# One decode step: a quarter of the scores of the first and the last head pair on TensorE, one load for w_mod, another order of work at the end

## The chip, the cores and the metric

One NeuronCore of one Trainium2 chip runs the whole program. The metric is the time of the execution on the device in microseconds (us). The kernel before took 685.55 us in the median of 3 runs (685.35 to 686.33).

## The reference: what is computed

A block for one token: adaptive layer norm, attention over a cache of 16384 keys and values for each of 32 heads of width 128, and a SwiGLU feed-forward part (width 640, inner width 1728). The core of it:

```python
mod = (silu(c) @ w_mod).reshape(1, 6, 1, 640)       # sa, ca, ga, sb, cb, gb
h = layernorm(x) * (1 + ca) + sa
q = (h @ wq) as 32 heads of 128
scores = q . k_cache[head] * 128 ** -0.5             # 32 x 16384
o = softmax(scores) @ v_cache[head]
x = x + ga * (o @ wo)
h = layernorm(x) * (1 + cb) + sb
x = x + gb * ((silu(h @ w_gate) * (h @ w_up)) @ w_down)
```

Almost all bytes are the two caches: 32 heads x 16384 x 128 x 2 bytes, twice, 268 MB of the 290.5 MB that the profile counts.

## The kernel before: tiles, loops and order

**Pairs.** The heads are worked in 16 pairs, u = 0 to 15. The keys of a pair are one tile `ks`: 128 partitions (64 for each head) with T2 = 256 tokens of 128 numbers each, 8.39 MB. The values of a pair have the same shape. Three slots of that size lie in the tile `big`; loads go through them in turn (k0, k1, v0, k2, v1, ..., k15, v14, v15), and a load waits until the slot's last user is done (`free_after`). w_mod lies in the slot that v0 takes later, wq in that of k1. At the end wo takes the slot of k15, and the feed-forward weights (`wg`, `wu`, `wd`) that of v14.

**Scores, on VectorE (DVE).** For each pair DVE multiplies the keys by the pair's query, which lies broadcast over the tokens in `qbc` (L540, in two pieces of 64 and 192 tokens, for pair 0 in four of 64), then adds halves of the 128 products: 128 to 64 to 32 (L543, L554), 32 to 16 (L556 for the first 32 tokens, L560 into the tile `F16` for the other 224), and reduces the last 16 to one score for each token in `S_v` (L558, L563). L565 takes the maximum. When L560 is done, the keys' slot is free (`o_kfree`).

**Softmax and values.** TensorE (PE) turns the maxima into a row (L443), DVE reduces it (L445), PE spreads it (L452), ScalarE (ACT) makes the bias (L455) and the exponentials (L459) into `P2`. This of pair u - 1 is placed after the first multiply of pair u. PE then multiplies probabilities by values (L484, 64 matmuls of 512 columns in a loop), ACT copies the sums out (L495) into the values' slot, and PE turns them (L503, `turn`); after that the slot is free (`o_vfree`). The last pair has its own form: 256 matmuls with a value tile as weights and two columns (L579).

**The end.** Group by group of 8 heads, the outputs are scaled (L513, `group_out`), spread (L518), and gathered (L522, L524) into `A_sb`; four groups of 40 matmuls with wo (L599) sum into `attn_ps`. Then the second layer norm (L326 to L338), gate and up (L655), and down (L673) in three pieces that wait for the loads of wd: blocks 0 to 5, 6 to 9, and 10 to 13. L679 to L685 make and store the output.

**The order is written by hand.** Every operation has an engine and a position; each engine's list is sorted by position, and each engine works its list strictly in that order. An operation waits for the last semaphore value of each dependency that its engine has not yet seen. DMAs are operations on the queue of SP (`plan.dma`, issued at L71), and a DMA that waits holds back those behind it. B = BU(u) and E = EU(u) are the positions of a pair's begin and end. The lines that the change touches are the load of w_mod (L283: one load of the columns 0 to 1279, and a second one, placed behind the keys of pair 0, of the rest; the second part is multiplied at L394, and only then v0 may be loaded), the loop over pairs (L526 to L569), and the end (L571 to L606).

Of the kernel before, what the change touches and what calls it, by code (L numbers as in the profile page):

```python
# [36 lines left out]
class _Plan:  # L37
# [104 lines left out]
def build(nc, A_x, A_k, A_v, A_wq, A_wo, B_wg, B_wu, B_wd, c_in, w_mod, out):  # L142
    H, S, Dh = A_k.shape[1], A_k.shape[2], A_k.shape[3]
    D = A_x.shape[2]
    F = B_wg.shape[1]
    assert Dh == 128 and D % 128 == 0 and S % 128 == 0
    KC = D // 128
# [5 lines left out]
    GQ = 4  # L153
    NU = H // 2
    T2 = 2 * TT
# [11 lines left out]
    def EU(u):  # L167
        return BU(u) + 37.2
# [8 lines left out]
    with es:  # L177
        block = es.enter_context(nc.Block())
        plan = _Plan(nc, es)

        def sb(name, shape, dtype):
            return es.enter_context(nc.sbuf_tensor(name, list(shape), dtype))
# [14 lines left out]
        wm_v = mat(2, 0, KC, 6 * D)  # L197
# [6 lines left out]
        TS = 32  # L204
# [4 lines left out]
        P2f = P2[:].rearrange("p t h -> p (t h)")  # L209
        ident_f = sb("ident_f", [128, 128], F32)  # L210
        ramp = F16[:].bitcast(F32).rearrange("p t c -> p (t c)")[:, 0:128]
        gm2 = sb("gm2", [1, 2], F32)
        one_f = sb("one_f", [128, 1], F32)
        one_bf = sb("one_bf", [128, 1], BF16)
# [65 lines left out]
        wq_src = A_wq.rearrange("(p k) n -> p k n", p=128)  # L280
        d_c = plan.dma(0.06, c_one, c_in, "c", name="dma_c", eng="act")
        d_x = plan.dma(0.07, x_one, A_x[0], "x", name="dma_x", eng="act")
        d_wm = [plan.dma(p_, wm_v[:, :, a:b], wm_src[:, :, a:b], ("wm", a), name="dma_wmod%d" % a) for p_, a, b in ((0.0, 0, 2 * D), (0.3, 2 * D, 6 * D))]  # L283
        d_wq = plan.dma(0.1, wq_v, wq_src, "wq", name="dma_wq")


# [71 lines left out]
        o_mod = op(PE, 2.0, lambda e: f_mod(e, wm_v, 0, 2, lambda o, k: slice(o + k, o + D, KC)), deps=[d_wm[0], o_sc], name="mod_mm_a")  # L358
# [32 lines left out]
        o_q_all = list(o_q.values())  # L391


        o_mod_b = op(PE, 4.5, lambda e: f_mod(e, wm_v, 2, 6, lambda o, k: slice(o + 128 * k, o + 128 * (k + 1))), deps=[d_wm[1], o_h], name="mod_mm_b")  # L394
        o_modc = op(ACT, 4.6, lambda e: e.activation(out=modb[:], in_=mod_ps[:, 2 * KC:6 * KC], func=ACTF.Copy), deps=[o_mod_b], name="mod_b")
        o_onep_b = op(DVE, BU(0) + 36.0, lambda e: e.tensor_scalar_add(out=onep_b[:], in0=modb[:, 2 * KC:3 * KC], scalar1=1.0), deps=[o_modc], name="onep_b")
        ga, sb_, gb = modb[:, 0:KC], modb[:, KC:2 * KC], modb[:, 3 * KC:4 * KC]
        o_gbx = op(DVE, BU(0) + 36.05, lambda e: e.tensor_copy(out=gbx, in_=gb), deps=[o_modc], name="gb_pairs")


        KV = {}
        for u in range(NU):
            KV["k", u], KV["v", u] = NK(u), NV(u)
# [34 lines left out]
            o_e8[n] = op(DVE, 1.83, f_e8, deps=[o_ident], name="e%d" % n)  # L438
        o_as = [None] * len(GROUPS)
        lnl_last = None  # L440

        def softmax(u, pos):
            o_T = op(PE, EU(u) + 0.1, lambda e: e.matmul(row_ps, lhsT=pm[:, u:u + 1], rhs=ident_f[:], start=True, stop=True),  # L443
# [83 lines left out]
        for u in range(NU):  # L527
            B, E = BU(u), EU(u)
            ks = tokens(KV["k", u])
            if u:  # L530
                d_v[u - 1] = load("v", u - 1, B - 1.0, [free_after(NV(u - 1))] if u > 1 else [o_mod_b])
                if u + 1 < NU:
                    d_k[u + 1] = load("k", u + 1, B - 0.9, [free_after(NK(u + 1))])
                else:
                    d_v[u] = load("v", u, B - 0.9, [free_after(NV(u))])
            cuts = [0, 64, 128, 192, T2] if u == 0 else [0, 64, T2]
            prev = []
            for c, (a, b) in enumerate(zip(cuts, cuts[1:])):
                qb = qbc[:, u].unsqueeze(1).broadcast_to([128, b - a, 128])
                prev.append(op(DVE, B + (6.0 if u == 0 else 4.5) * c, lambda e, ks=ks[:, a:b, :], qb=qb: e.tensor_tensor(out=ks, in0=ks, in1=qb, op=ALU.mult),  # L540
                               deps=[d_k[u][c if u == 0 else 0], o_qbc[u]], name="mult%d_%d" % (u, c)))
                if u == 0:
                    prev[c] = op(DVE, B + 6.0 * c + 4.0, lambda e, ks=ks[:, a:b, :]: e.tensor_tensor(  # L543
                        out=ks[:, :, 0:64], in0=ks[:, :, 0:64], in1=ks[:, :, 64:128], op=ALU.add), deps=[prev[c]], name="fold64_%d_%d" % (u, c))
                elif c == 0:
                    softmax(u - 1, B + 4.0)
                    if u % 2 == 0:
                        sums(u // 2 - 1, B + 4.2)
                    if u >= 3 and u % 2 == 1:
                        group_out(2 * u - 6, GQ, B + 4.3, o_diag[u - 2])  # L550
            w = 64 if u == 0 else 128
            while w > 32:
                w //= 2
                prev = [op(DVE, E - 14.0 + 0.1 * (8 - math.log2(w)), lambda e, ks=ks, w=w: e.tensor_tensor(  # L554
                    out=ks[:, :, 0:w], in0=ks[:, :, 0:w], in1=ks[:, :, w:2 * w], op=ALU.add), deps=prev, name="fold%d_%d" % (w, u))]
# [4 lines left out]
            o_kfree[u] = op(DVE, E - 6.0, lambda e, ks=ks: e.tensor_tensor(  # L560
                out=F16[:], in0=ks[:, TS:, 0:16], in1=ks[:, TS:, 16:32], op=ALU.add),
                deps=prev + [o_ra, o_ident], name="fold16_%d" % u)
            o_red[u] = op(DVE, E - 4.0, lambda e: e.tensor_reduce(out=S_v[:, TS:], in_=F16[:], axis=AX.X, op=ALU.add),  # L563
                          deps=[o_kfree[u]], name="red%d" % u)
            o_max[u] = op(DVE, E - 0.5, lambda e, u=u: e.tensor_reduce(out=pm[:, u:u + 1], in_=S_v[:], axis=AX.X, op=ALU.max),  # L565
                          deps=[o_red[u]], name="max%d" % u)
            if u:
                value(u - 1, B + 19.0)
                turn(u - 1, E + 0.15)  # L569

        softmax(NU - 1, EU(NU - 1) + 0.2)  # L571
        sums(H // GQ - 1, EU(NU - 1) + 0.3)
        group_out(H - 4, 2, EU(NU - 1) + 0.5, o_diag[NU - 2])
        vl = tokens(KV["v", NU - 1])

        def f_pvl(e):
            last = None
            for t in range(T2):
                last = e.matmul(OTL[:, 0:2], lhsT=vl[:, t, :], rhs=P2[:, t, :], start=(t == 0), stop=(t == T2 - 1))  # L579
            return last  # L580
        o_pv[NU - 1] = op(PE, EU(NU - 1) + 1.2, f_pvl, deps=[o_exp[NU - 1], d_v[NU - 1][0], o_acc[NU - 3]], name="pv%d" % (NU - 1))
        group_out(H - 2, 2, EU(NU - 1) + 1.5, o_pv[NU - 1])


# [150 lines left out]
```

## Time and profile before

| what | value |
|---|---|
| profiled execution | 684.71 us, of which the span 682.9 us |
| median of the runs | 685.55 us (3 runs) |
| DVE busy | 616.4 us (90%) |
| PE busy | 318.8 us (47%) |
| ACT busy | 52.4 us (8%) |
| HBM read | 290.47 MB, 425 GB/s over the span |
| keys of pair 0: first and last multiply begin | 24.77 us, 44.76 us |
| keys of pair 15: first multiply begins | 610.89 us |
| last matmul of down ends | about 680.5 us |

The span is the time between the first and the last instruction of the profiled execution. A line of the timeline gives start, duration, engine, line, operation, tiles, how many instructions are merged, and in brackets the idle time before and what ended it. "PE" is the matmul, "PEld" the load of its weights; "SPq" is the issue of a DMA. "DMA share" is the mean busy share of the 16 DMA engines.

### The profile page before, as it was taken

The page shows a single profiled execution, that of the slowest core. Times are in us where ns is not written, and L with a number is a line of the kernel's source. Part 1 is how long each engine was busy: PE and PEld are TensorE (multiplying, and loading weights), DVE is VectorE, ACT ScalarE, POOL GpSimd, SP SyncE. Part 2 cuts the span into 40 slices and gives each one's busy share as a digit, 9 for nine tenths or more (in the row PEclk, how much of TensorE's full clock was granted, in tenths as well). Part 3 has the DMA queues.
Part 4 walks back from the last instruction along what each step waited for, and adds up shares of the span by engine and source line. Part 5 has one row for each costly group of instructions (what it writes and reads, how often), then busy time and mean ns, then how long its engine had stood idle before and what let it go on. Part 6 is the DMA issues. An engine that isn't in the chain of part 4 may idle for free.

```text
span 682.9 us, 5976 instructions
## 1 busy us (share of the span) xinstructions
PE 318.8 (47%) x2037; PEld 149.0 (22%) x2038; DVE 616.4 (90%) x215; ACT 52.4 (8%) x179; POOL 0.2 (0%) x4
## 2 busy tenths in 40 slices
PE   2610082643718182562709174451709264371866
PEld 2210031211303131120303022120303122130365
DVE  2597999999999999999999999999999999999901
ACT  1300001010010101010010101001010101001010
POOL 0000000000000000000000000000000000000000
PEclk9955585775858586675959576685958577585955
DMA  8999999999999999999999999999999999999996
GB/s 365 425 451 434 449 427 434 430 419 430 430 438 430 434 430 435 430 434 430 430 430 430 434 438 427 438 430 438 438 438 430 430 441 431 434 430 430 402 416 259
DMA packets 9420, 290.68 MB, mean 426 GB/s; under 512 B 764, under 2 KB 958, under 8 KB 4286
## 3 DMA queue, kind: packets, MB, share of 16 engines
q1 hardware_dynamic: 9402, 290.48, 98.9%
q8 instruction: 10, 0.16, 0.1%
q14 instruction: 4, 0.03, 0.0%
q10 hardware_dynamic: 4, 0.00, 0.0%
HBM read 290.47 MB, written 0.00 MB: 425 GB/s over the span
## 4 chain that ended last, share of the span: by engine, by line
DMA 46%; DVE 41%; PE 7%; issue 6%; ACT 0%; SPq 0%; DVEq 0%
DMA big<-in_A_k_cache_dram 44%; DVE big L540 16%; DVE big L554 15%; DVE S_v L563 5%; DMA big<-in_A_wq_dram 3%; DVE F L560 2%; PE psb L376 2%; PE psb L503 1%; PE psb L579 1%; DVE S_v L558 1%; PE psb L599 1%; PE psb L655 1%; DVE big L556 1%; DVE pm L565 1%; PE psb L443 0%
## 5 line engine op out<-in xcount | busy, mean ns | idle before, releaser
L484 PE MATMUL psb<-big,P 128*8 (+1 forms) x960 | 243.1, 421 | 192.8 <-DMA big<-in_A_v_cache_dram 192.8
L540 DVE TENSOR_TENSOR big<-big,qbc 128x8192 bf16<-128x8192 bf16 (+1 forms) x34 | 278.1, 8179 | 23.3 <-DMA big<-in_A_k_cache_dram 23.3
L554 DVE TENSOR_TENSOR big<-big 128x8192 bf16<-128x8192 bf16 (+1 forms) x31 | 201.2, 6490 | 1.1
L484 PEld LDWEIGHTS psb<-big,P 128*8 (+1 forms) x960 | 89.1, 93 | 340.6 <-DMA big<-in_A_v_cache_dram 121.6
L563 DVE TENSOR_REDUCE S_v<-F 128x224 f32<-128x3584 bf16 x16 | 62.2, 3886 | 0.5
L495 ACT ACTIVATE big<-psb 8x512 f32<-8x512 f32 x15 | 8.8, 587 | 421.5 <-PE psb L484 421.5
L560 DVE TENSOR_TENSOR F<-big 128x3584 bf16<-128x3584 bf16 x16 | 32.4, 2024 | 0.6
L443 PE MATMUL psb<-ident_f,pm 128*1 128x128 f32 x32 | 7.1, 311 | 53.1 <-DVE pm L565 53.1
L452 PE MATMUL psb<-gm,one_f 1*64 1x1 f32 x64 | 5.9, 248 | 54.5 <-DVE gm L445 54.5
L503 PE MATMUL psb<-ident_f,big 8*128 8x2 f32 x120 | 20.9, 292 | 0.0
L503 PEld LDWEIGHTS psb<-ident_f,big 8*128 8x128 f32 x120 | 19.7, 244 | 4.2 <-issue 4.2
L459 ACT ACTIVATE P<-S_v,nb 64x256 bf16<-64x256 f32 x32 | 18.5, 578 | 0.7
L452 PEld LDWEIGHTS psb<-gm,one_f 1*64 1x64 f32 x64 | 4.6, 196 | 56.2 <-DVE gm L445 56.2
L443 PEld LDWEIGHTS psb<-ident_f,pm 128*1 128x1 f32 x32 | 1.4, 81 | 60.7 <-DVE pm L565 60.7
L376 PE MATMUL psb<-big,h_col 128*128 128x512 bf16 x39 | 10.4, 434 | 8.2 <-DMA big<-in_A_wq_dram 8.2
L354 PE MATMUL psb<-silu_c,big 128*128 128x1 bf16 x150 | 5.0, 170 | 17.9 <-DMA big<-in_w_mod_dram 17.9
L455 ACT ACTIVATE nb<-psb 128x1 f32<-128x1 f32 x16 | 2.7, 171 | 131.6 <-PE psb L452 131.6
L513 DVE TENSOR_TENSOR on_f<-psb,rl 128x4 f32<-128x4 f32 (+1 forms) x9 | 1.3, 144 | 11.6 <-PE psb L579 8.0
L558 DVE TENSOR_REDUCE S_v<-big 128x32 f32<-128x512 bf16 x16 | 11.0, 686 | 0.6
L467 PE MATMUL psb<-rs,one_f 128*128 128x4 f32 x16 | 4.7, 366 | 12.5 <-ACT P L459 12.5
L543 DVE TENSOR_TENSOR big<-big 128x4096 bf16<-128x4096 bf16 x4 | 9.2, 2292 | 0.1
L354 PEld LDWEIGHTS psb<-silu_c,big 128*128 128x128 bf16 x150 | 4.8, 113 | 18.4 <-DMA big<-in_w_mod_dram 18.4
(84 smaller groups left out, 105.5 us busy)
## 6 DMA issues: line engine op xcount, KB each, us to landing
big<-in_A_k_cache_dram SPq DMA_DIRECT2D x4, 2048.0 KB, 30.5
big<-in_A_wq_dram SPq DMA_DIRECT2D x1, 5120.0 KB, 18.4
big<-in_A_wo_dram SPq DMA_DIRECT2D x1, 3840.0 KB, 14.5
big<-in_w_mod_dram SPq DMA_DIRECT2D x1, 3200.0 KB, 44.4
big<-in_B_w_gate_dram SPq DMA_DIRECT2D x1, 2160.0 KB, 16.9
big<-in_B_w_up_dram SPq DMA_DIRECT2D x1, 2160.0 KB, 21.8
big<-in_w_mod_dram SPq DMA_DIRECT2D x1, 1600.0 KB, 7.0
big<-in_A_wo_dram SPq DMA_DIRECT2D x1, 1280.0 KB, 17.0
```

What stands on the lines that cost most here:

```text
L354: last = e.matmul(mod_ps[:, m * KC + k:m * KC + k + 1], lhsT=wv[:, kd, cols(m * D, k)], rhs=silu_c[:, kd:kd + 1], start=(kd == 0), stop=(k ...
L376: last = e.matmul(q_ps[b][:, 0:n * 128], lhsT=h_col[:, k:k + 1].broadcast_to([128, 128]), rhs=wv[:, k, n0:n0 + n * 128], start=(k == 0), s ...
L452: last = e.matmul(top_ps[64 * hh:64 * hh + 64, :], lhsT=one_f[0:1, :].broadcast_to([1, 64]), rhs=gm2[:, hh:hh + 1], start=True, stop=True)
L459: o_exp[u] = op(ACT, pos + 0.03 + 0.01 * hh, lambda e, p_=p_, hh=hh: e.activation(out=P2[p_, :, hh], in_=S_v[p_, :], func=ACTF.Exp, scale= ...
L484: return e.matmul(acc_ps[b][0:8, :], lhsT=P2f[:, bass.ds(t, 8)], rhs=big[:, bass.ds(at, 512)], start=start, stop=stop)
L503: last = e.matmul(OT_ps[:, 2 * u:2 * u + 2], lhsT=acc_v[:, 128 * i:128 * (i + 1)], rhs=ident_f[0:8, 2 * i:2 * i + 2], start=(i == 0), stop ...
L540: prev.append(op(DVE, B + (6.0 if u == 0 else 4.5) * c, lambda e, ks=ks[:, a:b, :], qb=qb: e.tensor_tensor(out=ks, in0=ks, in1=qb, op=ALU. ...
L543: prev[c] = op(DVE, B + 6.0 * c + 4.0, lambda e, ks=ks[:, a:b, :]: e.tensor_tensor(out=ks[:, :, 0:64], in0=ks[:, :, 0:64], in1=ks[:, :, 64 ...
L554: prev = [op(DVE, E - 14.0 + 0.1 * (8 - math.log2(w)), lambda e, ks=ks, w=w: e.tensor_tensor(out=ks[:, :, 0:w], in0=ks[:, :, 0:w], in1=ks[ ...
L558: o_ra = op(DVE, E - 6.1, lambda e, ks=ks: e.tensor_reduce(out=S_v[:, 0:TS], in_=ks[:, 0:TS, 0:16], axis=AX.X, op=ALU.add), deps=[o_fa] + ...
L560: o_kfree[u] = op(DVE, E - 6.0, lambda e, ks=ks: e.tensor_tensor(out=F16[:], in0=ks[:, TS:, 0:16], in1=ks[:, TS:, 16:32], op=ALU.add), dep ...
L563: o_red[u] = op(DVE, E - 4.0, lambda e: e.tensor_reduce(out=S_v[:, TS:], in_=F16[:], axis=AX.X, op=ALU.add), deps=[o_kfree[u]], name="red% ...
```

## The change

- **w_mod** comes in one load, the first of SP's queue, instead of two; both uses wait for it.
- **Pairs 0 and 15:** the last 64 of the 256 tokens are left out of all DVE steps (`nt` = 192 instead of 256). Their scores are made in `scores_pe`: PE turns the pair's query into two columns (one for each head), and 8 times over, PE transposes 8 tokens' keys into a PSUM bank (two banks in turn), ACT copies the 1024 columns into a third of `F16` as bf16, and PE multiplies each 128 x 128 tile with the two query columns. Two ACT copies then put the scores into `S_v`. In pair 0 this stands on PE behind the second part of the w_mod product; in pair 15 behind the softmax of pair 14 and ahead of the values of pair 14. DVE's step into `F16` (L560) waits for the two copies, since `F16` is their buffer.
- **The end:** on PE the turn of pair 14 comes behind the spread of pair 15's maximum, not ahead of it. The 256 matmuls of pair 15 are cut at token 192; the sums of the last four heads and the gathering of heads 28 and 29 stand between the pieces. The feed-forward loads move by 0.05 in position, to stay behind that turn.

The diff, cut to its core:

```diff
-        d_wm = [plan.dma(p_, wm_v[:, :, a:b], wm_src[:, :, a:b], ("wm", a), name="dma_wmod%d" % a) for p_, a, b in ((0.0, 0, 2 * D), (0.3, 2 * D, 6 * D))]
+        d_wm = plan.dma(0.0, wm_v, wm_src, "wm", name="dma_wmod")
...
+        TX = 64
+        SHARED = (0, NU - 1)
...
+        XT = 8
+        X0 = T2 - TX
+        kt = F16[:].rearrange("p t c -> p (t c)")
+        kt_ps = [st_ps[:].bitcast(BF16), f_ps[:].bitcast(BF16)]
+        o_xs = {}
+
+        def scores_pe(u, pos, ks, c, f_free):
+            o_qcm = op(PE, pos, lambda e: e.matmul(attn_ps[:, 16:18], lhsT=qbc[:, u, :], rhs=ident[:, 0:128:64], start=True, stop=True),
+                       deps=[o_qbc[u], o_ident, o_xf1], name="q_columns%d" % u)
+            o_qc = op(ACT, pos + 0.01, lambda e: e.activation(out=q_col[:], in_=attn_ps[:, 16:18], func=ACTF.Copy), deps=[o_qcm], name="q_col%d" % u)
+            NX = TX // XT
+            mm, ev = [], []
+            for i in range(NX):
+                t0 = X0 + XT * i
+                ps, buf = kt_ps[i % 2], kt[:, 128 * XT * (i % 3):128 * XT * (i % 3 + 1)]
+
+                def f_tr(e, t0=t0, ps=ps):
+                    last = None
+                    for j in range(XT):
+                        last = e.transpose(ps[:, 128 * j:128 * (j + 1)], ks[:, t0 + j, :], ident[:])
+                    return last
+                o_tr = op(PE, pos + 0.1 + 0.2 * i, f_tr, deps=[d_k[u][c], o_ident, ev[i - 2] if i >= 2 else f_free], name="k_tr%d_%d" % (u, i))
+                ev.append(op(ACT, pos + 0.15 + 0.2 * i, lambda e, ps=ps, buf=buf: e.activation(out=buf, in_=ps[:, 0:128 * XT], func=ACTF.Copy),
+                             deps=[o_tr, mm[i - 3] if i >= 3 else f_free], name="k_cols%d_%d" % (u, i)))
+
+                def f_mm(e, i=i, buf=buf):
+                    last = None
+                    for j in range(XT):
+                        o = 64 + 2 * (XT * i + j)
+                        last = e.matmul(attn_ps[:, o:o + 2], lhsT=buf[:, 128 * j:128 * (j + 1)], rhs=q_col[:], start=True, stop=True)
+                    return last
+                mm.append(op(PE, pos + 0.4 + 0.2 * i, f_mm, deps=[ev[i], o_qc], name="k_scores%d_%d" % (u, i)))
+            sp = attn_ps[:, 64:64 + 2 * TX].rearrange("p (t h) -> p t h", h=2)
+            for hh in range(2):
+                p_ = slice(64 * hh, 64 * hh + 64)
+                o_xs[u] = op(ACT, pos + 0.5 + 0.2 * NX + 0.01 * hh, lambda e, p_=p_, hh=hh: e.activation(out=S_v[p_, X0:], in_=sp[p_, :, hh], func=ACTF.Copy),
+                             deps=[mm[-1]] + ([o_exp[u - 1]] if u else []), name="s_part%d_%d" % (u, hh))
...
+            nt = T2 - TX if u in SHARED else T2
+            cuts = [0, 64, 128, 192] if u == 0 else [0, 64, nt]
+            if u == 0:
+                scores_pe(u, 4.6, ks, 3, o_cc)
+            if u == NU - 1:
+                scores_pe(u, B + 5.0, ks, 0, o_red[u - 1])
...
-                deps=prev + [o_ra, o_ident], name="fold16_%d" % u)
+                deps=prev + [o_ra, o_ident, o_xs.get(u)], name="fold16_%d" % u)
...
-                turn(u - 1, E + 0.15)
+                turn(u - 1, E + (0.15 if u < NU - 1 else 0.25))
...
-        sums(H // GQ - 1, EU(NU - 1) + 0.3)
-        group_out(H - 4, 2, EU(NU - 1) + 0.5, o_diag[NU - 2])
...
+        for i, (a, b) in enumerate(((0, 192), (192, T2))):
...
+            o_pv[NU - 1] = op(PE, EU(NU - 1) + 0.6 + 0.3 * i, f_pvl, deps=[o_exp[NU - 1], d_v[NU - 1][0], o_acc[NU - 3]], name="pv%d_%d" % (NU - 1, i))
+            if i == 0:
+                sums(H // GQ - 1, EU(NU - 1) + 0.7)
+                group_out(H - 4, 2, EU(NU - 1) + 0.8, o_diag[NU - 2])
...
-        TW = EU(NU - 1) + 0.4
+        TW = EU(NU - 1) + 0.45
```

More of the change, by code (lines that the diff above doesn't have):

```diff
@@ L211, in build @@
         ramp = F16[:].bitcast(F32).rearrange("p t c -> p (t c)")[:, 0:128]
+        q_col = sb("q_col", [128, 2], BF16)
         gm2 = sb("gm2", [1, 2], F32)
@@ L357, in f_mod @@
             return last
-        o_mod = op(PE, 2.0, lambda e: f_mod(e, wm_v, 0, 2, lambda o, k: slice(o + k, o + D, KC)), deps=[d_wm[0], o_sc], name="mod_mm_a")
+        o_mod = op(PE, 2.0, lambda e: f_mod(e, wm_v, 0, 2, lambda o, k: slice(o + k, o + D, KC)), deps=[d_wm, o_sc], name="mod_mm_a")
         o_t1 = op(DVE, 2.1, lambda e: e.scalar_tensor_tensor(
@@ L391, in build @@
         o_q_all = list(o_q.values())
-        o_mod_b = op(PE, 4.5, lambda e: f_mod(e, wm_v, 2, 6, lambda o, k: slice(o + 128 * k, o + 128 * (k + 1))), deps=[d_wm[1], o_h], name="mod_mm_b")
+        o_mod_b = op(PE, 4.5, lambda e: f_mod(e, wm_v, 2, 6, lambda o, k: slice(o + 128 * k, o + 128 * (k + 1))), deps=[d_wm, o_h], name="mod_mm_b")
         o_modc = op(ACT, 4.6, lambda e: e.activation(out=modb[:], in_=mod_ps[:, 2 * KC:6 * KC], func=ACTF.Copy), deps=[o_mod_b], name="mod_b")
@@ L535, in build @@
                     d_v[u] = load("v", u, B - 0.9, [free_after(NV(u))])
-            cuts = [0, 64, 128, 192, T2] if u == 0 else [0, 64, T2]
+            nt = T2 - TX if u in SHARED else T2
[4 more added lines that the diff above has]
+                scores_pe(u, B + 5.0, ks, 0, o_red[u - 1])
             prev = []
@@ L553, in build @@
                 w //= 2
-                prev = [op(DVE, E - 14.0 + 0.1 * (8 - math.log2(w)), lambda e, ks=ks, w=w: e.tensor_tensor(
+                prev = [op(DVE, E - 14.0 + 0.1 * (8 - math.log2(w)), lambda e, ks=ks[:, 0:nt, :], w=w: e.tensor_tensor(
                     out=ks[:, :, 0:w], in0=ks[:, :, 0:w], in1=ks[:, :, w:2 * w], op=ALU.add), deps=prev, name="fold%d_%d" % (w, u))]
@@ L559, in build @@
                       deps=[o_fa] + ([o_exp[u - 1]] if u else []), name="reda%d" % u)
-            o_kfree[u] = op(DVE, E - 6.0, lambda e, ks=ks: e.tensor_tensor(
-                out=F16[:], in0=ks[:, TS:, 0:16], in1=ks[:, TS:, 16:32], op=ALU.add),
-                deps=prev + [o_ra, o_ident], name="fold16_%d" % u)
-            o_red[u] = op(DVE, E - 4.0, lambda e: e.tensor_reduce(out=S_v[:, TS:], in_=F16[:], axis=AX.X, op=ALU.add),
+            o_kfree[u] = op(DVE, E - 6.0, lambda e, ks=ks, nt=nt: e.tensor_tensor(
+                out=F16[:, 0:nt - TS], in0=ks[:, TS:nt, 0:16], in1=ks[:, TS:nt, 16:32], op=ALU.add),
+                deps=prev + [o_ra, o_ident, o_xs.get(u)], name="fold16_%d" % u)
+            o_red[u] = op(DVE, E - 4.0, lambda e, nt=nt: e.tensor_reduce(out=S_v[:, TS:nt], in_=F16[:, 0:nt - TS], axis=AX.X, op=ALU.add),
                           deps=[o_kfree[u]], name="red%d" % u)
@@ L568, in build, with f_pvl @@
                 value(u - 1, B + 19.0)
-                turn(u - 1, E + 0.15)
+                turn(u - 1, E + (0.15 if u < NU - 1 else 0.25))
         softmax(NU - 1, EU(NU - 1) + 0.2)
-        sums(H // GQ - 1, EU(NU - 1) + 0.3)
-        group_out(H - 4, 2, EU(NU - 1) + 0.5, o_diag[NU - 2])
         vl = tokens(KV["v", NU - 1])
[L576 to L581, printed above, removed]
+        for i, (a, b) in enumerate(((0, 192), (192, T2))):
+            def f_pvl(e, a=a, b=b):
+                last = None
+                for t in range(a, b):
+                    last = e.matmul(OTL[:, 0:2], lhsT=vl[:, t, :], rhs=P2[:, t, :], start=(t == 0), stop=(t == T2 - 1))
+                return last
+            o_pv[NU - 1] = op(PE, EU(NU - 1) + 0.6 + 0.3 * i, f_pvl, deps=[o_exp[NU - 1], d_v[NU - 1][0], o_acc[NU - 3]], name="pv%d_%d" % (NU - 1, i))
+            if i == 0:
+                sums(H // GQ - 1, EU(NU - 1) + 0.7)
+                group_out(H - 4, 2, EU(NU - 1) + 0.8, o_diag[NU - 2])
         group_out(H - 2, 2, EU(NU - 1) + 1.5, o_pv[NU - 1])
```

## The prediction, made before the changed kernel was run

> **What bounds the kernel now.** I read the profile page's rows over 40 slices and its chain first, then the timeline of the first 75 us and of the last 125 us.
>
> ```profile
> DMA  8999999999999999999999999999999999999996
> ...
> DMA 46%; DVE 41%; PE 7%; issue 6%; ACT 0%; SPq 0%; DVEq 0%
> ```
>
> The DMA engines are full from the second slice to the last but one. DVE is 90% busy, but it follows: its own wait for keys is short and comes back in every pair. Keys land every 38.7 us (the multiplies of pairs 1, 3, 5 begin at 67.89, 145.33, 222.74 us; half of 77.4), which is 16.78 MB at 433 GB/s, while DVE needs 38.3 us for a pair (572.04 to 610.3). So DMA bounds the middle, DVE has some 0.5 us to spare in each pair, and two ends are left: how soon the stream of bytes is through, and what comes after its last byte. The first end, in the timeline:
>
> ```profile
> 63.18 0.41 DVE L565 TENSOR_REDUCE pm<-S_v 128x1 f32<-128x256 f32 x1
> ...
> 67.89 4.43 DVE L540 TENSOR_TENSOR big<-big,qbc 128x8192 bf16<-128x8192 bf16 x1 [4.30 <-DMA big<-in_A_k_cache_dram]
> ```
>
> DVE is through with pair 0 at 63.6 and sits 4.30 us until the keys of pair 1 are in. Work taken from DVE here only makes that wait longer. The last end:
>
> ```profile
> 630.36 16.20 PE L484 MATMUL psb<-big,P 128*8 128x512 bf16 x64 [14.42 <-DMA big<-in_A_v_cache_dram]
> ...
> 649.30 0.38 PE L443 MATMUL psb<-ident_f,pm 128*1 128x128 f32 x2 [2.74 <-DVE pm L565]
> ...
> 652.87 5.07 PE L579 MATMUL psb<-P,big 128*128 128x2 bf16 x185
> ...
> 659.63 2.05 PE L579 MATMUL psb<-P,big 128*128 128x2 bf16 x71 [1.68 <-issue]
> ...
> 665.55 1.84 PE L599 MATMUL psb<-A_sb,big 128*128 128x1 bf16 x63 [2.36 <-issue]
> ...
> 672.39 4.43 PE L655 MATMUL psb<-h_col,big 128*128 128x1 bf16 x140 [1.04 <-DVE h_col L639]
> ...
> 677.16 0.32 PE L673 MATMUL psb<-gu_col,big 128*128 128x1 bf16 x6 [0.34 <-DVE gu_col L664]
> 678.59 1.93 PE L673 MATMUL psb<-gu_col,big 128*128 128x1 bf16 x64 [1.12 <-issue]
> ```
>
> ```profile
> 678.00:679.00 1.00, 0.41 (x16) 0.41 (x16) 0.00 (x0) 0.00 (x0) 0.00 (x0) 0.50 0.00 0
> ```
>
> From 649.3 on PE works in a chain with three gaps put down to "issue": 1.68, 2.36 and 1.12 us. The DMA view of short stretches has one 16 KB instruction packet near each, and 128 matmuls (71 + 57) lie between the first two gaps, so 256 instructions with their weight loads: I read them as waits for PE's next page of instructions. A page comes 5.4 us (654.2, where the page before began at 27 ns a matmul, to 659.6) to 5.9 us (659.6 to 665.55) after the page before began. The last window is the point: no byte moves after 678, yet down works until 680.5. The last load (80 KB of wd, issued 667.4, landed 11.1 us later, at 678.5) leaves 20 matmuls of 30 ns, 0.6 us. So the end could be at 679.1; the PE chain holds it 1.45 us longer.
>
> **The change, part by part.**
>
> *w_mod in one load.* Its row pieces of 2560 and 5120 bytes become one of 38.4 KB for each partition. Two stretches that hold such pieces only, by the DMA view (packets, MB, share):
>
> ```profile
> q1 hardware_dynamic: 330, 0.84, 90.7%
> ```
>
> ```profile
> q1 hardware_dynamic: 329, 1.68, 103.4%
> ```
>
> 0.85 MB in 2.5 us at 90.7% is 373 GB/s when full, and 1.68 MB in 4 us at 103.4% is 406. So 1.638 MB / 373 + 3.277 MB / 406 = 12.45 us now, and 4.915 MB at 432 (wq and caches) = 11.4: the stream is 1.05 us shorter. Bounds: 0 (the gaps hidden elsewhere; a loss is excluded, since wq's pieces of 41 KB run at 432) and 1.5 (the first stretch at its plain 338). The first products start later: wq lands 7 us later (19.85 to 26.8), the first multiply at 31.7 instead of 24.77. This is covered in pair 0 (below). The load of v0 may go when the second product is done, now near 40.5 instead of 51.4; it is needed at 67. No gain there. The little load of x (landed 4.58) now shares the engines with larger pieces; it is needed for h near 16, so even some us cost nothing.
>
> *Pair 0.* DVE loses one multiply (4.42), one fold (2.29), a quarter of 4.43, 2/7 of 2.02 and of 3.89: 9.5 us. From 31.7: three times 6.69, then 3.3, 0.42, 0.69, gives 56.3. L560 then waits for the scores from PE. These start when the keys are in (40.5 now, plus 7 = 47.5). A round is 8 transposes, an ACT copy, 8 matmuls. No row shows a stream of transposes. Above: the single one at L683 takes 0.27 us, so 2.2 for 8. Below: 128 of the 512 columns that L484 streams warm (10.45 us for 49, 53 ns), 0.43. I take the slow rate of L484 (430 ns for 512, so 107) with 27 ns of a weight load from L579: 1.07 for 8, since a stream is the nearer likeness. The 8 matmuls as in L579: 0.22. The copy: L383 (256 elements) 378 ns, L495 (512) 587, so 0.82 ns each, 1.0 us for 1024, beside PE. A round is 1.35 us with 0.06 for hand-overs, and all of it 1.07 + 1.0 + 7 x 1.35 + 0.25 + 0.6 (two copies) = 12.4: ready at 60. Then 1.44, 2.78, 0.6: DVE is done at 65, and pair 1's keys come at 66.8. **Nothing gained, nothing lost**; if it takes longer, the next pairs make up 0.5 us each, and SP's loads have spare time (v1 is issued at 101.8, needed at 105.5).
>
> The Trainium skill ("TensorE: Matmul & The Clock Gate", PE-mode transpose) speaks against this: it gives some 275 ns for a 128 x 128 transpose in a kernel. If each really took that in a stream, a round would be 2.6 us by my estimate from that page, and the third rival would be the forecast; no row here shows such a stream.
>
> *Pair 15.* DVE is 9.4 us sooner with the maximum: near 639 instead of 649.2 (keys at 609.9, from 38.4 to 29 us). PE's rounds start when ACT has done the exponentials and the four spreads of pair 14 (now 618.4, so 617.3) and end near 628.5. Only then come pair 14's values, whose load lands at 629.3 (now 630.3). So they start on time, and end at 645.1. L443 is queued behind them: **PE's value work, not DVE, is late next**. From L443 to the end of the exponentials takes 3.1 now (649.3 to 652.4), 1.0 of it the turn that moves behind: 2.6 with a margin, 647.7. v15 lands near 648.8 (19.4 us, half of 38.7, after v14). The last product starts at 648.9, not 652.7. wo is issued some 9 us sooner and wg 3 us, but both queue behind v15, so no byte comes sooner for it.
>
> *The end.* The sums of the last heads (L467, 0.59 on PE) move from ahead of the last product into it; their scale and spread run on ACT and DVE beside its second piece and are needed first by L522, behind three groups of wo. Cost nothing; without that cover, 1.3 us (L467 to L518 now, 652.4 to 653.8). PE gets 2 x 129 more matmuls, 516 instructions, two pages and 4: the pages begin where they began, within some matmuls. So from 648.9: pages at 650.4, then 655.9 (5.5 later), 661.8 (5.9). Rest of wo 3.4 us, layer norm 3.45: gate at 668.7, 3.7 sooner. wu lands at 671.9 (651.1 + 21.8 less 1.05), so up ends near 674, down starts at 674.5, and the next page (669.1 + 5.7) is in at 674.8. Down is then held by the last wd: 678.5 less what the stream saves, plus 0.6.
>
> *Two more pages* are two more 16 KB packets, each near 1 us on one DMA engine. Around the four pages of the middle, keys came 0, 0.4, 0 and 0.7 us late, so I take 0.3 each (bounds 0 and 1.0). The stream saves 1.05 - 0.6 = 0.45, up to 1.05.
>
> **Sum.** End of down now 680.55; after: 678.5 - 0.5 + 0.6 = 678.6. That is 1.95 less (2.5 without the pages' cost): span 680.9, execution 682.7 instead of 684.71. The runs' median lies 0.84 above the profiled execution, so 685.55 - 2.0 = **683.5**. Some 0.2% (1.4 us) is about what a measurement of this kernel can tell from no change.
>
> **Rivals.**
> 1. *The tail gives it back, about 685.0.* For: three page waits of 1.1 to 2.4 us stand there now, and one that falls into the last 20 matmuls costs all of it. Against: 516 is two pages and 4. The stream may also save nothing (small pieces hidden, page fetches on the slowest engine): 679.1 + 0.6 is a gain of 0.9 only, 684.7. Both within 0.2%.
> 2. *All of w_mod's saving arrives and nothing is lost:* 2.5 to 3, 682.7.
> 3. *Slower: transposes take their single time.* A round of 2.6 us ends pair 15's scores at 617.3 + 22 = 639, so pair 14's values end at 655, and the tail starts 7 us later than now instead of 3.7 sooner; pair 0's scores end at 69, DVE is 7 late for pair 1, v1 is issued some 4 us too late. Near 695. It turns slower from a round of 2.1 us: then the values of pair 14 start 5 us late, which uses up 1.1 (v15), 1.2 (wd) and the gain. For: L683. Against: everything PE streams here starts at the rate of its columns.
>
> **Chances.** Forecast 0.50 and rival 2 0.12, both faster by over 0.2%; rival 1 0.27, within; slower 0.11, of it the transposes 0.08. The range goes from 682.4 (the stream's full 1.05, and a little of the rest) to 686.2, which leaves out the slower cases and the edges of the others.
>
> **What would show it.** w_mod's packets at 430 GB/s and k1 in at 66.8; DVE's wait there; rounds of 1.35 us; the values of pair 14 starting with their load; the last product at 648.9; a page gap or none in down; no byte after 677.5 to 678 and down's end 0.6 later. Wrong if the rounds take over 2 us, or if a page wait stands in the last 20 matmuls.

## The result and the profile after

The changed kernel takes 683.13 us in the median of 9 runs (682.51 to 684.95), the kernel before 685.78 beside it (9 runs, 684.84 to 686.43). The ratio is 0.9967, with a 95% interval of 0.9956 to 0.9979: 2.3 us faster, between 1.4 and 3.0. The forecast was 2.0. The profiled execution is one of 683.13 us with a span of 681.3 us, 1.6 us under that of before (682.9).

The same rows of the profile page of the changed kernel as were shown of before:

```profile
DMA  9999999999999999999999999999999999999997
...
DMA 51%; DVE 39%; PE 5%; SPq 3%; ACT 1%; issue 0%; DVEq 0%
```

The chain's largest part is now DMA by more: 51% instead of 46%. The fall of "issue" from 6% to 0% says little about the tail: of some 38 us of "issue" before, the three gaps of PE's tail are 5.2 (1.68, 2.36 and 1.12), and seven stretches of about 4 us beside multiplies of the middle are most of the rest. What tells is how the chain ends. The last load of wd and the 20 matmuls behind it stand there now, and PE's gaps are off it (start, duration, what):

```profile
667.27 10.74 DMA big<-in_B_w_down_dram
...
678.06 0.80 PE psb L720 x20
```

The first end, in the timeline of the changed kernel:

```profile
31.63 4.43 DVE L585 TENSOR_TENSOR big<-big,qbc 128x8192 bf16<-128x8192 bf16 x1 [14.44 <-DMA big<-in_A_k_cache_dram]
...
47.46 1.89 PE L463 MATMUL psb<-ident,big 128*128 128x128 bf16 x16 [7.93 <-DMA big<-in_A_k_cache_dram]
...
56.28 0.35 PE L473 MATMUL psb<-q_col,F 128*128 128x2 bf16 x8 [0.20 <-ACT F L466]
...
58.16 1.49 DVE L605 TENSOR_TENSOR F<-big 128x2560 bf16<-128x2560 bf16 x1 [1.89 <-ACT S_v L479]
...
62.56 0.41 DVE L610 TENSOR_REDUCE pm<-S_v 128x1 f32<-128x256 f32 x1
...
66.84 4.42 DVE L585 TENSOR_TENSOR big<-big,qbc 128x8192 bf16<-128x8192 bf16 x1 [3.87 <-DMA big<-in_A_k_cache_dram]
```

DVE begins the first multiply at 31.63 instead of 24.77. The transposes (L463) begin when the last keys of pair 0 are in, and the scores are copied at 58.1; DVE's step L605 waits 1.89 us for them. The keys of pair 1 come 1.05 us sooner than before (66.84, 67.89), and DVE still waits 3.87 us for them. The last end:

```profile
629.95 15.92 PE L524 MATMUL psb<-big,P 128*8 128x512 bf16 x64 [2.97 <-DMA big<-in_A_v_cache_dram]
...
638.80 0.42 DVE L610 TENSOR_REDUCE pm<-S_v 128x1 f32<-128x256 f32 x1
...
645.71 0.38 PE L483 MATMUL psb<-ident_f,pm 128*1 128x128 f32 x2
...
649.39 4.98 PE L623 MATMUL psb<-P,big 128*128 128x2 bf16 x185 [1.68 <-DMA big<-in_A_v_cache_dram]
...
656.66 0.35 PE L623 MATMUL psb<-P,big 128*128 128x2 bf16 x7 [2.29 <-issue]
...
662.60 1.89 PE L646 MATMUL psb<-A_sb,big 128*128 128x1 bf16 x65 [1.98 <-issue]
...
669.50 2.24 PE L702 MATMUL psb<-h_col,big 128*128 128x1 bf16 x70 [1.04 <-DVE h_col L686]
...
672.65 2.25 PE L702 MATMUL psb<-h_col,big 128*128 128x1 bf16 x70 [0.91 <-DMA big<-in_B_w_up_dram]
...
675.24 1.09 PE L720 MATMUL psb<-gu_col,big 128*128 128x1 bf16 x30 [0.34 <-DVE gu_col L711]
...
676.64 0.69 PE L720 MATMUL psb<-gu_col,big 128*128 128x1 bf16 x20 [0.31 <-DMA big<-in_B_w_down_dram]
...
678.06 0.79 PE L720 MATMUL psb<-gu_col,big 128*128 128x1 bf16 x20 [0.73 <-DMA big<-in_B_w_down_dram]
```

The maximum (L610) is there at 639.2, but the row of it (L483) stands on PE behind the values of pair 14 until 645.7. The last product (L623) begins 3.5 us sooner than before and is released by the load of v15, not by PE. Its page gaps are still there (2.29 and 1.98 us). The gap in down is not: up and the last two pieces of down are released by their loads. The time is now the last wd load plus 0.8 us for the 20 matmuls behind it.

### The profile page after: what moved, and what is told of

The parts are those of the page before. It is cut to its first block, busy times and chain, and to the rows that moved or that the text cites. A ratio compares the mean times of both kernels' runs of the same rounds, so it can differ in the third digit from the quotient of the medians.

```text
span 681.3 us, 6514 instructions
## 1 busy us (share of the span) xinstructions
PE 337.8 (50%) x2296; PEld 165.1 (24%) x2296; DVE 598.0 (88%) x213; ACT 69.2 (10%) x201; POOL 0.2 (0%) x4
## 4 chain that ended last, share of the span: by engine, by line
DMA 51%; DVE 39%; PE 5%; SPq 3%; ACT 1%; issue 0%; DVEq 0%
DMA big<-in_A_k_cache_dram 46%; DVE big L585 18%; DVE big L599 14%; DMA big<-in_A_v_cache_dram 4%; DVE S_v L608 3%; SPq L71 3%; PE psb L524 2%; DVE F L605 2%; DMA big<-in_B_w_down_dram 2%; PE psb L543 1%; ACT F L466 1%; DVE S_v L603 1%; DVE big L601 0%; PE psb L483 0%; PE psb L463 0%
## 5 line engine op out<-in xcount | busy, mean ns | idle before, releaser
L585 DVE TENSOR_TENSOR big<-big,qbc 128x8192 bf16<-128x8192 bf16 (+2 forms) x33 | 269.4, 8164 | 25.1 <-DMA big<-in_A_k_cache_dram 25.1
L599 DVE TENSOR_TENSOR big<-big 128x16384 bf16<-128x16384 bf16 (+3 forms) x31 | 196.9, 6352 | 1.1
L608 DVE TENSOR_REDUCE S_v<-F 128x224 f32<-128x3584 bf16 (+1 forms) x16 | 60.0, 3753 | 0.5
L605 DVE TENSOR_TENSOR F<-big 128x3584 bf16<-128x3584 bf16 (+1 forms) x16 | 31.3, 1958 | 2.4 <-ACT S_v L479 1.9
L483 PE MATMUL psb<-ident_f,pm 128*1 128x128 f32 x32 | 6.9, 302 | 42.8 <-DVE pm L610 42.8
L543 PE MATMUL psb<-ident_f,big 8*128 8x2 f32 x120 | 21.3, 295 | 0.0
L463 PE MATMUL psb<-ident,big 128*128 128x128 bf16 x128 | 14.9, 295 | 7.9 <-DMA big<-in_A_k_cache_dram 7.9
L466 ACT ACTIVATE F<-psb 128x1024 bf16<-128x1024 bf16 x16 | 15.9, 1020 | 10.6 <-PE psb L463 10.4
L463 PEld LDWEIGHTS psb<-ident,big 128*128 128x128 bf16 x128 | 11.7, 134 | 8.0 <-DMA big<-in_A_k_cache_dram 8.0
L483 PEld LDWEIGHTS psb<-ident_f,pm 128*1 128x1 f32 x32 | 1.4, 81 | 50.2 <-DVE pm L610 49.9
L485 DVE TENSOR_REDUCE gm<-psb 1x2 f32<-1x128 f32 x16 | 4.4, 272 | 6.9 <-PE psb L483 6.9
```

Of the source, the lines that this page charges most:

```text
L463: last = e.transpose(ps[:, 128 * j:128 * (j + 1)], ks[:, t0 + j, :], ident[:])
L466: ev.append(op(ACT, pos + 0.15 + 0.2 * i, lambda e, ps=ps, buf=buf: e.activation(out=buf, in_=ps[:, 0:128 * XT], func=ACTF.Copy), deps=[o_ ...
L605: o_kfree[u] = op(DVE, E - 6.0, lambda e, ks=ks, nt=nt: e.tensor_tensor(out=F16[:, 0:nt - TS], in0=ks[:, TS:nt, 0:16], in1=ks[:, TS:nt, 16 ...
L608: o_red[u] = op(DVE, E - 4.0, lambda e, nt=nt: e.tensor_reduce(out=S_v[:, TS:nt], in_=F16[:, 0:nt - TS], axis=AX.X, op=ALU.add), deps=[o_k ...
```

## The experiments

The theory at the start: **two ends.** The time is the later of the stream's end (last wd load, and 0.8 us) and PE's chain in the tail. Rival A: the work taken from DVE, the busiest engine, is what counts. Rival B: the shorter stream is all. All kernels ran beside the kernel before (685.5 us in the median of each series), 5 to 12 runs each; the intervals reach 0.6 to 1.0 us to each side, so half a microsecond can't be told from nothing. For each kernel stand the ratio to before, its 95% interval, and the median.

The changed kernel did not run again in these series. "More than the changed kernel" compares with its 683.13 above, whose ratio has the interval 0.9956 to 0.9979. The runs tell a kernel from it only where the intervals lie apart: w_mod alone, pair 0 on DVE alone, the front alone, the order alone, and the two with the shorter value loop. The other differences from it are medians side by side and are not shown by the runs.

In the profiled executions the keys of pair 15 came between 609.9 and 612.8 us (twelve kernels with the old value loop), so the place where one of them ends says little. Two distances say more. *The front:* the keys of pair 1 begin at 67.8 to 68.2 in the four kernels with w_mod in two loads, and at 66.8 to 67.1 in the six of the twelve with one load in which DVE waits for them, 1.05 us apart in the mean. *The tail,* from the keys of pair 15 to the end of down: 69.0 to 70.1 us in the five kernels that leave pair 15 to DVE, and in none of these do the last matmuls of down wait for a load; 68.4 to 68.9 in the five that share 64 of its tokens and load wd as before, and in all of these the last 20 wait for wd. So the tail is 0.9 us shorter in the mean, and its bound went from PE's chain to the last load.

**Only w_mod in one load, in the kernel before.**

```diff
-        d_wm = [plan.dma(p_, wm_v[:, :, a:b], wm_src[:, :, a:b], ("wm", a), name="dma_wmod%d" % a) for p_, a, b in ((0.0, 0, 2 * D), (0.3, 2 * D, 6 * D))]
+        d_wm = plan.dma(0.0, wm_v, wm_src, "wm", name="dma_wmod")
...
```

(and both uses wait for this load.)

> The kernel before, with only w_mod's one load added. Theory of the two ends (the time is the later of the last wd load and PE's chain): the stream is about 1 us shorter, the keys of pair 1 land at 66.8 instead of 67.9, DVE begins pair 0 7 us later and is 3.8 us late for pair 1, makes up 0.5 us a pair, and the whole tail comes 1 us sooner: 1 us faster than before, 684.7. Rival A (DVE's work is what counts): 3 us or more slower, since DVE is late and nothing is taken from it. Rival B (the shorter stream is the whole gain): 2.6 us faster.

Measured: 1.0020 (1.0006 to 1.0034), 687.21 us: 1.4 us slower by the ratio. All three expectations missed it. DVE was late for pair 1 as expected (70.51), but then v1 was issued too late. The timeline of SP and DVE in this kernel:

```profile
70.51 4.42 DVE L540 TENSOR_TENSOR big<-big,qbc 128x8192 bf16<-128x8192 bf16 x1
...
104.43 0.33 SPq L71 DMA_DIRECT2D big<-in_A_v_cache_dram  x1
...
108.69 4.42 DVE L540 TENSOR_TENSOR big<-big,qbc 128x8192 bf16<-128x8192 bf16 x1
```

and the busy time of each engine in the stretch from 99 to 109 us (the last two columns are DMA share and GB/s), of this kernel and then of the changed one:

```profile
99.00:109.00 10.00, 3.66 (x18) 1.27 (x16) 9.83 (x7) 0.59 (x1) 0.00 (x0) 0.91 0.82 323
```

```profile
99.00:109.00 10.00, 6.06 (x28) 3.16 (x25) 9.51 (x4) 0.59 (x1) 0.00 (x0) 0.79 0.95 400
```

In the changed kernel v1 is issued at 100.77 and the share is 0.95; here it is issued at 104.43, with the keys of pair 2 already in, and the share is 0.82. By the packet records all but one or two of the 16 engines stand idle together from 104.2 to 105.2, and the idle time is 1.7 us in the mean over the engines. That is more than the 1.05 us that w_mod saves. Keys are from then on later than in the changed kernel (pair 5 at 223.69, not 221.64). The theory had to be mended: **w_mod whole and the sharing of pair 0 are one measure**. The first shortens the stream and makes DVE 7 us late; the second repays DVE.

**The changed kernel with w_mod in two loads.** The edit is the reverse of the one above.

> The changed kernel, with w_mod in two loads again. Theory of the two ends: the stream is 0.5 to 1 us longer and holds the end, so 0.5 to 1 us slower than the changed kernel (683.6 to 684.1); the tail still waits for the last wd load. Rival A: no difference. Rival B: all the gain gone, 685.8.

Measured: 0.9973 (0.9962 to 0.9984), 683.69 us, 0.56 more than the changed kernel. Down's end waits for its load as expected:

```profile
678.48 0.78 PE L720 MATMUL psb<-gu_col,big 128*128 128x1 bf16 x20 [0.95 <-DMA big<-in_B_w_down_dram]
```

That is 0.4 us later than in the changed kernel (678.06), and the keys of pair 1 are 0.94 later (67.78). Rival B's 685.8 is out. The intervals of the two kernels overlap, so the size of this part is not shown by the run times, and the 0.4 us rests on one execution of each.

**The changed kernel with pair 0 on DVE alone.**

```diff
-        SHARED = (0, NU - 1)
+        SHARED = (NU - 1,)
...
-            cuts = [0, 64, 128, 192] if u == 0 else [0, 64, nt]
-            if u == 0:
-                scores_pe(u, 4.6, ks, 3, o_cc)
+            cuts = [0, 64, 128, 192, T2] if u == 0 else [0, 64, nt]
```

> The changed kernel, with pair 0 on DVE alone again. Theory of the two ends: no difference within 0.3 us; DVE is done with pair 0 near 70.5, begins pair 1 some 3.7 us late, and is back at waiting for keys after some eight pairs; one instruction page fewer. Rival A: 3 us or more slower than the changed kernel.

Measured: 1.0000 (0.9988 to 1.0013), 685.46 us: 2.3 us more, all the gain. The theory failed here in the same place: DVE begins pair 1 at 70.58, v1 is issued at 104.50, and the DMA engines run dry for 1.8 us in the mean. Rival A's number is nearer, but not for its reason: the kernel with only the tail, below, has no sharing of pair 0 either and keeps half the gain, with w_mod in two loads.

**The changed kernel with pair 15 on DVE alone.**

```diff
-        SHARED = (0, NU - 1)
+        SHARED = (0,)
...
-            if u == NU - 1:
-                scores_pe(u, B + 5.0, ks, 0, o_red[u - 1])
```

> The changed kernel, with pair 15 on DVE alone again. Theory of the two ends: the maximum comes at 648.3, the last product starts near 650.9 instead of 649.4, gate near 670.6, and PE's chain ends near 678.8, where the last wd load ends it too: 0 to 0.5 us slower than the changed kernel. Rival A: back to 685 or more.

Measured: 0.9984 (0.9975 to 0.9993), 684.53 us, 1.4 more than the changed kernel, where 0 to 0.5 was expected. In its profile PE's chain ends last, as expected, but at 681.0 instead of the 678.8 that I worked out: the keys of pair 15 came 1.8 us later in this execution than in the changed kernel's (611.73), and the page gap is back in down:

```profile
677.78 0.30 PE L718 MATMUL psb<-gu_col,big 128*128 128x1 bf16 x5 [0.34 <-DVE gu_col L709]
678.97 2.03 PE L718 MATMUL psb<-gu_col,big 128*128 128x1 bf16 x65 [0.89 <-issue]
```

**Only the front, only the tail, only the order.** The front is w_mod whole and pair 0 shared; the tail is pair 15 shared and the new order; the order is the new order alone, in the kernel before. The edits are the parts of the diff.

> Only the front part of the change: w_mod whole and pair 0 shared; pair 15 on DVE alone and the end's order as before. Theory as mended (w_mod whole takes 1 us off the stream but makes DVE 3.7 us late for pair 1, so that v1 is issued too late and the DMA engines run dry for 1.7 us; sharing pair 0 pays that back): the engines do not run dry, keys of pair 1 at 66.8, the whole tail 0.5 to 1 us sooner, 684.5 to 685.0, with PE's chain still ending last. Rival (the end's order and pair 15 do it all): 685.5.

> Only the tail part of the change: pair 15 shared and the end's new order; w_mod in two loads and pair 0 on DVE alone. Theory: with DVE begun at 24.8 as before, pair 0 needs no sharing; the tail is held by the last wd load near 678.5, so 683.3 to 683.8, as the kernel with two loads and both pairs shared (683.69). Rival (pair 0's sharing is worth 2 us by itself): 685.5.

> The kernel before with only the end's new order (turn of pair 14 behind the spread, the last product cut at token 192, loads moved by 0.05). Theory: the exponentials come 1.0 us sooner, since the turn takes 1.05 us on PE ahead of the spread; PE's chain ends 0.5 to 1 us sooner: 684.5 to 685.0. Rival (the order is worth nothing, or the later feed-forward loads cost): 685.5 or more.

Measured: front 0.9993 (0.9982 to 1.0004), 685.17 us; tail 0.9978 (0.9968 to 0.9988), 684.31 us; order 0.9992 (0.9981 to 1.0002), 684.79 us. So the front alone is within noise of nothing, 0.3 us; the tail alone brings 1.2 (0.5 to 1.0 less than I expected); the whole 2.3 to 2.6. In the profile of the front alone the engines do not run dry and the keys of pair 1 come at 67.09, as expected, and PE's chain ends last; but the keys of pair 15 come at 612.40, 1.5 us later than in the kernel before. In that of the tail alone down's last two pieces wait for their loads, as expected; the last one begins at 680.00, with the keys of pair 15 at 612.36. Why the medians miss the expectations by these amounts is open. That a shorter stream is worth less while PE's chain ends last is not shown: the chain begins with loads of the same stream, and 0.3 us alone and 1.2 beside the tail are not told apart by these runs. On the way through the middle the 1.05 us of the front are lost in the scatter: at the keys of pair 15 the six kernels with one load are no sooner in the mean than the four with two (611.4 us both). So the saving of w_mod is shown at pair 1 and is open at the end. The order alone is not clear of nothing in the runs; in its profile the last product begins 2.6 us after the row of the maximum (650.06 to 652.65) instead of 3.6, which is the turn's 1.0.

**The changed kernel with the old order at the end.**

```diff
-                turn(u - 1, E + (0.15 if u < NU - 1 else 0.25))
+                turn(u - 1, E + 0.15)
...
-        TW = EU(NU - 1) + 0.45
+        TW = EU(NU - 1) + 0.4
```

(and the last product in one piece, with the sums ahead of it.)

> The changed kernel with the end's old order. Theory: the turn goes ahead of the spread again, 1.05 us on PE, but the values of pair 15 land only 1.2 us after the exponentials in the changed kernel, so this is hidden, and later the loads of wu and wd hold the end: no difference from the changed kernel within 0.4 us, 682.8 to 683.5. Rival (each microsecond of PE's chain counts): 1 us slower, 684.1.

Measured: 0.9964 (0.9951 to 0.9976), 683.38 us: not told apart from the changed kernel, as expected. Its tail lasts 68.5 us from the keys of pair 15, that of the changed kernel 68.9. Once pair 15 is shared, the new order has nothing to give that these runs show.

**128 tokens of pair 15 on TensorE.**

```diff
-        X0 = T2 - TX
...
+            TX = 64 if u == 0 else 128
+            X0 = T2 - TX
             NX = TX // XT
...
-            nt = T2 - TX if u in SHARED else T2
+            nt = T2 - (64 if u == 0 else 128) if u in SHARED else T2
```

> The changed kernel with 128 instead of 64 tokens of pair 15 on TensorE and ScalarE (pair 0 as before it, 64). Theory (PE's value work, not DVE's maximum, is what the tail waits for): 16 rounds of 1.27 us end near 638, the values of pair 14 start 7.8 us later than their load, the last product near 656, gate near 676, and PE's chain ends 5 to 6 us later: 688 to 689. Rival (DVE's maximum is what the tail waits for): DVE is another 9 us sooner, so the same time or less, 683 or below.

Measured: 0.9985 (0.9975 to 0.9994), 684.63 us, 1.5 more than the changed kernel: the sign is the theory's, the size a third of what I wrote. The tail bears the sign out: 70.4 us from the keys of pair 15, 1.7 more than the mean of the kernels with 64 tokens. Its profiled execution is the longest of its ten (687.36; the row of pair 14's maximum stands at 612.42, in the changed kernel at 609.57), but what waits for what is plain:

```profile
637.50 0.35 PE L474 MATMUL psb<-q_col,F 128*128 128x2 bf16 x8 [0.56 <-ACT F L467]
637.78 15.11 PE L525 MATMUL psb<-big,P 128*8 128x512 bf16 x64
...
641.32 0.42 DVE L611 TENSOR_REDUCE pm<-S_v 128x1 f32<-128x256 f32 x1
...
652.73 0.38 PE L484 MATMUL psb<-ident_f,pm 128*1 128x128 f32 x2
```

DVE's maximum is there at 641.7 and waits 11 us for PE. The values of pair 14 begin right behind the scores. The size was off in part because the later rounds are quicker: eight transposes take 1.01 us at first, where the granted clock is 0.50, and 0.61 from the eleventh round on, where it is 1.00 (from 630.0), so that the ACT copy (1.0 us) sets the pace, and the values, at a clock of 1.00 from their start, take 15.1 us and not 15.9.

```profile
628.64 1.01 PE L464 MATMUL psb<-ident,big 128*128 128x128 bf16 x8
...
632.92 0.61 PE L464 MATMUL psb<-ident,big 128*128 128x128 bf16 x8
```

**A better tail.** wd in pieces of 6, 4 and 2 rows, and the last block alone behind the last wait:

```diff
-        WD_CUTS = [0, 6, 2 * NP2 - 2]
+        WD_CUTS = [0, 6, 10, 13]
...
-                dst = wd_v[:, a:b, :].rearrange("p (j i) n -> p j (i n)", i=2)
-                src = B_wd[128 * a:128 * b, :].rearrange("(j p i) n -> p j (i n)", p=128, i=2)
+                dst = wd_v[:, a:b, :].rearrange("p i n -> p (i n)")
+                src = B_wd[128 * a:128 * b, :].rearrange("(p i) n -> p (i n)", p=128)
...
-                        cols = slice(256 * (j // 2) + j % 2, 256 * (j // 2 + 1), 2)
+                        a, b = [g for g in ((0, 6), (6, 10), (10, 12)) if g[0] <= j < g[1]][0]
+                        cols = slice(128 * a + j - a, 128 * b, b - a)
```

> The changed kernel with wd loaded in pieces of 6, 4 and 2 rows for each partition instead of 2, 2 and 2, and with down's last piece cut again, so that only 5 matmuls instead of 20 wait for the last load. Theory (the last wd load holds the end): the stream is some 0.3 to 0.4 us shorter and 15 matmuls of 0.03 us move ahead of the last wait, 0.7 to 0.9 us less than the changed kernel: 682.2 to 682.5. Rival (PE's chain holds the end): no difference, 683.1.

Measured: 0.9965 (0.9954 to 0.9977), 683.04 us: not told apart from the changed kernel. In its profile the last byte is in 0.6 us sooner and down ends 0.8 us sooner (678.06 instead of 678.85), though its last 20 matmuls still run as one piece behind one wait, where 5 were expected; gate and up, whose columns now lie 6, 4 and 2 apart, take 2.96 us each instead of 2.25:

```profile
668.89 2.96 PE L703 MATMUL psb<-h_col,big 128*128 128x1 bf16 x70 [1.04 <-DVE h_col L686]
...
677.28 0.78 PE L721 MATMUL psb<-gu_col,big 128*128 128x1 bf16 x20 [0.36 <-DMA big<-in_B_w_down_dram]
```

Its tail lasts 67.5 us from the keys of pair 15, the shortest of all. By the profile it is the better kernel, by the runs it is open.

**A shorter value loop.**

```diff
-        PVB, PVT = 6, (T2 // 4 - 1) // 6
+        PVB, PVT = 2, (T2 // 4 - 2) // 2
```

> The changed kernel with the value loop's body cut from 6 to 2 matmuls (31 turns instead of 10), which takes 16 instructions of PE from each of 15 pairs, 240 in all. Theory (every 16 KB page of PE's instructions is a packet on one DMA engine, and the keys come 0 to 1.6 us late where one falls into the middle): one page fewer in the middle, 0.5 us less in the median, 682.6, with the keys late in two places instead of three; and the first gap of the last product stands after 177 matmuls instead of 185 (240 is 16 short of a page). If the shorter loop costs PE its pace, the values of pair 14 take over 17 us and the last product starts later. Rival (page fetches are harmless, the late keys have another cause): the same late keys at the same three places, the gap after 185, 683.1.

> Both of the former edits in one kernel. Theory: both add up, 1.2 us less than the changed kernel, 681.8. Rival: 683.1 or no better than the better one of the two.

Measured: 1.0248 (1.0217 to 1.0279), 701.78 us, and with the wd edit 1.0263 (1.0244 to 1.0282), 704.45 us: 18.7 and 21.3 us more than the changed kernel. The part of the expectation with "if" came true and drowned the rest. Two turns of the loop in the timeline of PE:

```profile
107.18 0.71 PE L524 MATMUL psb<-big,P 128*8 x2 [0.26 <-issue]
108.15 0.71 PE L524 MATMUL psb<-big,P 128*8 x2 [0.26 <-issue]
```

A turn of two matmuls takes 0.8 to 0.97 us, with 0.20 to 0.26 of it idle, so 31 turns take 25 to 30 us instead of 16; the values' slot comes free late, and the loads of keys wait. One thing it did settle: the first gap of the last product stands where it was reckoned from 240 instructions, after 177 matmuls and not 185:

```profile
672.98 4.87 PE L623 MATMUL psb<-P,big 128*128 128x2 bf16 x177 [0.58 <-ACT P L499]
...
680.90 0.56 PE L623 MATMUL psb<-P,big 128*128 128x2 bf16 x15 [3.05 <-issue]
```

So the gaps are tied to the count of PE's instructions, 256 to a page. What a page costs the stream could not be tried this way. What the profiles give: in 12 profiled executions of kernels with the old loop, the keys of pairs 2 to 15 come 38.70 us apart where nothing happens. In 46 intervals in which a page packet of PE ran they came 0 to 1.71 us late, 0.42 in the mean; in 114 without one 0.04. That the page packet is the cause is likely and not shown.

## Why the prediction was right, point by point

| step | forecast | measured |
|---|---|---|
| first multiply of DVE | 31.7 | 31.63 |
| keys of pair 1 | 66.8 | 66.84 |
| DVE through with pair 0 | 65 | 63.0 |
| scores of pair 15 done on PE | 628.5 | 627.0 |
| values of pair 14 begin, end | 629.3, 645.1 | 629.95, 645.7 |
| last product begins | 648.9 | 649.39 |
| page waits end | 655.9, 661.8 | 656.66, 662.60 |
| gate, down begin | 668.7, 674.5 | 669.50, 675.24 |
| last wd load in | 678.0 | 678.06 |
| down ends | 678.6 | 678.86 |

*The tail was right in its mechanism, and near in its size.* After DVE's maximum it is PE's value work that is late; v15, wu and wd then hold PE; no page wait is left in down; the end is the last load and 0.8 us. In this profile the stream's end came 0.5 us sooner by the last wd load, which is the value I took (1.05 saved, half of it given back). That this agrees so well is partly luck, as the keys of pair 15 differ by up to 2.9 us between the profiled executions. Here it was still 0.95 sooner at the keys of pair 15 (609.94, 610.89) and 0.4 at v14 (629.95, 630.36); that the giving back is the pages' doing stays likely only. The load of w_mod itself ran as forecast: its packets took 1.42 us, 433 GB/s, but for the first 16 with some 2.1. The measured gain in the runs, 2.3 to 2.65, is above the forecast 2.0; the two profiled executions differ by 1.6. Executions of the changed kernel lie up to 2.4 us apart, those of the kernel before up to 4.2 in one series, so the rest is not worked out further.

*The rounds were priced nearly right, for the slow rate.* I took 1.35 us from the streamed rows L484 and L579. In pair 15 of the changed kernel, at a granted clock of 0.50, two rounds take 2.37 us while eight transposes take 1.01, so 1.19 each; with transposes at 0.61, as in the kernel with 128 tokens at a clock of 1.00, eight copies follow each other in 7.75 us, and ACT sets the pace. The mean recorded duration of one transpose is 295 ns, near the single one of L683 (270) and near the 275 ns that the Trainium skill gives ("TensorE: Matmul & The Clock Gate", PE-mode transpose). It is the time from start to end of one, not the distance between two: eight stand in 1.01 us. Going by it, as the third rival did, would have given some 695. (The third rival's own times put the tail 5 to 6 us later than before, 655 against 649.3 for the row of the maximum, and not the 7 that it names.)

*One step of pair 0 was wrong*, though the sum did not show it: "if it takes longer, the next pairs make up 0.5 us each, and SP's loads have spare time (v1 is issued at 101.8, needed at 105.5)". v1 is needed when the engines are through with the keys of pair 2. In the kernel with w_mod alone they ran out of packets from 103.5 on; v1 was issued at 104.43, and its first packets came about a microsecond later, from 105.4 on. With DVE 3.7 us late the engines ran dry for 1.7 us. So "nothing gained, nothing lost" holds against the kernel before, but the sharing of pair 0 is worth 2.3 us in the medians where w_mod comes whole (the intervals lie apart); I had both halves of that, the 7 us delay and the slack of v1, and priced the slack by the landing of the load ahead of it instead of its last byte.

*The rivals.* The tail did not give it back, since 516 more instructions leave the pages where they were (the first gap stands after 185 matmuls in both kernels) and no page wait falls into the last 20 matmuls. The transposes are no bound at 64 tokens: the values of pair 14 wait for their load (2.97 us), not for the scores. At 128 tokens the scores end later than that load, and the tail is 1.7 us longer.

## What to carry to other kernels

In a kernel that streams all the time, a load queue has slack only up to the last byte of the load ahead of it, less the time from issue to first packet (about 1 us here); an edit that makes the consuming engine late is paid there, even if that engine catches up later. Find both ends of the tail, the last load and the compute chain, before pricing an edit: what is taken from one is worth only the distance to the other. Try the parts of a change in pairs: w_mod whole alone was 1.4 us slower here, and with pair 0 shared beside it 0.3 us faster, which the runs can't tell from nothing. And where single executions differ by more than the gain, compare distances inside each profile, as from the keys of pair 15 to the end.

## What the runs showed of the hardware that was not expected

- In the value loop, a body of 2 matmuls of 512 columns leaves PE idle for 0.20 to 0.26 us in each turn (0.8 to 0.97 us a turn); the 64 matmuls of a pair take 25 to 30 us, and with a body of 6 they take 15.1 to 16.9.
- PE's instructions come in pages of 256. In the tail of the twelve kernels with the old value loop, PE stands 1.6 to 2.6 us at each of the first two page boundaries, with 128 short matmuls between them, and goes on 5.9 to 6.2 us after it did at the boundary before. The Trainium skill ("Runtime: NRT & Kernel Launch", Instruction fetch mechanics) calls the crossing of a page mostly hidden; in this tail it is hidden only where PE waits for something else.
- Weight tiles whose columns lie 6, 4 or 2 apart take 42 ns a matmul in the mean in gate and up (2.96 us for 70), those with columns 2 apart 32 ns (2.25). In both the last two of the 14 blocks lie close.
- Eight transposes of 128 x 128 in a row take 1.01 us at a granted clock of 0.50 and 0.61 at 1.00 (the kernel with 128 tokens).
